# Casting the values on another engine and reordering the first batch of a fused attention and mixer kernel

## The chip, the cores and the metric

The kernel runs on one core of a Trainium2 chip. The metric is the device time of one execution in microseconds (us). The engines are named as in the profile: PE (TensorE, the matrix engine; PEld is its weight load), ACT (ScalarE), DVE (VectorE), POOL (GpSimd) and SP (SyncE, which here only issues transfers). Each engine works through its own instructions in the order in which they were written.

## The reference

For 8 batches of 12 heads, 448 tokens and head size 64:

```python
q_n, k_n = rmsnorm(q, g_q), rmsnorm(k, g_k)
attn = softmax(q_n @ k_n^T / 8)
x    = attn @ v                      # heads side by side: 448 x 768 per batch
u    = x + (x^T @ U @ V)^T           # low-rank mixing over tokens, rank 32
out  = u + relu(u @ w_ch1) @ w_ch2   # 768 -> 3072 -> 768
```

Inputs and output are float32; the kernel multiplies in bfloat16.

## The kernel before, in words

The 12 heads of a batch are worked in three groups of four heads, and a group is two pairs of heads, so a batch has six pairs. Groups are numbered over all batches: groups 0, 1 and 2 are batch 0, group 3 is the first of batch 1. A group goes through these steps:

- `load_qk` and `load_v` (lines 92 to 115) issue its q, k and v loads from SP. Three groups of tiles exist (`stage`, three buffers).
- `squares` (ACT or POOL), `sums` (DVE) and `roots` (ACT: a logarithm and an exponential, lines 169 and 170) make one over the root mean square of each row, in the tile `rs`. `scale` (line 173) multiplies q and k by it and writes `qn` and `kp` in bfloat16. `qn` and `kp` have one buffer each.
- `turn(gi, 0)` and `turn(gi, 1)` transpose `qn` and `kp` on PE (7 transposes each, line 354) into a PSUM tile `pt`. `take_q` and `take_k` (lines 357 and 366) copy them, on DVE, to `qT` and `kT`.
- `values(gi)` (line 199) casts v from float32 to bfloat16: one cast of 128x768 into `va` (line 201) and two of 64x128 into `vl` (line 203).

Then, for each pair, `Sc` (line 401) makes four blocks of scores on PE, r = 0 to 3, and ACT takes their exponential `E` (line 416): three of 128x896 and one of 128x448. Two PSUM tiles are there for scores, so a block can start when the exponential of two blocks earlier has been read. `V` (line 425) multiplies E with `va` and `vl` on PE for one half of the tokens; DVE takes the reciprocal of the row sums and scales the result (lines 444 and 445). In the tables, `V2(i, half)` is V for pair i.

Batch 0 is written out by hand. Its order is the dictionary `extra` (line 607): after each score block (pair, r) come the steps listed there. Ahead of it stand the first steps (lines 748 to 787), which also issue the loads of U, V and of group 3. `keep_busy(n)` issues n small matmuls on PE whose result nobody reads. `weights(n)` issues the next n loads of w_ch1 and w_ch2 from POOL's own queue (`load_w1`, line 276, four parts; then `load_w2`). `mix_t0`, `mix`, `mix_rows` do the low-rank mixing of batch 0; they need `prep_u` and `prep_v` (casts on POOL). All small PSUM tiles (`pt`, `pv`, `busy`, `pu` and others) share four buffers.

From the end of batch 0's attention on, the loop at line 822 takes turns between attention of the later batches (`att`) and the two large matmul stages `up` (line 529) and `down` (line 561), by costs and due times. It counts from the end of batch 0, so that the order of all that follows is the same before and after the change.

## Time and profile before

| what | value |
|---|---|
| median of 3 runs | 588.72 us (587.82 to 588.96) |
| the profiled execution, its time | 588.72 us |
| the profiled execution, its span | 586.8 us |
| PE busy, of the span | 574.6 us (98%) |
| ACT, POOL and DVE busy | 300.1, 213.3 and 197.1 us |
| PE busy from 0 to 44 us | 37.86 us |
| PE busy from 44 us to the end | 536.73 us of 543 |
| granted PE clock | 0.998 |

The span runs from the first to the last instruction; 1.92 us of the time lie around it. The page's first part gives busy time by engine. The timeline gives, for one engine and a window, start, duration, line, tile written and read, and in brackets the idle time before with what ended it; instructions of the same kind are merged ("x3"). Durations of POOL are rough.

### The profile page before, as it was taken

To read this page: it belongs to the slowest core of one execution; us is meant where nothing else is said; L and a number is where in the kernel's file an instruction comes from. 1 tells how busy PE (TensorE), PEld (TensorE's weight loads), DVE (VectorE), ACT (ScalarE), POOL (GpSimd) and SP (SyncE) were. 2 spreads that over 40 slices of the span, in tenths; PEclk is the share of its full clock that TensorE was granted. 3 is DMA by queue.
4 is the path that set the end of the run, shared out by engine and by line. 5 is a ranking of instruction groups with operands and counts; after the bars stand their busy time and mean duration, and the time that the engine had idled before them with its cause. 6 is when DMAs were issued, how large, how long until landed. Compare 5 with 4: busy or idle time off the path is not lost.

```text
span 586.8 us, 11702 instructions
## 1 busy us (share of the span) xinstructions
PE 574.6 (98%) x4826; PEld 334.2 (57%) x4826; DVE 197.1 (34%) x458; ACT 300.1 (51%) x472; POOL 213.3 (36%) x312
## 2 busy tenths in 40 slices
PE   8899999999999999999999999999999999999996
PEld 7655556555565555655566555655556555655563
DVE  6676655312353223521244330641134210410011
ACT  6866650678443774566744568347653254014200
POOL 5995684464044524415153605343352000000000
PEclk9999999999999999999999999999999999999999
DMA  8899999573536641775066732566024110420022
GB/s 222 168 241 241 244 234 220 125 192 75 133 76 170 150 121 26 179 179 124 6 156 105 189 93 55 142 171 146 10 46 103 41 28 1 62 67 1 1 54 55
DMA packets 104509, 68.21 MB, mean 116 GB/s; under 512 B 66568, under 2 KB 101256, under 8 KB 104456
## 3 DMA queue, kind: packets, MB, share of 16 engines
q1 hardware_dynamic: 95044, 58.03, 42.3%
q0 software_dynamic: 9408, 9.44, 9.6%
q8 instruction: 38, 0.62, 0.4%
q14 instruction: 15, 0.12, 0.1%
q10 hardware_dynamic: 4, 0.00, 0.0%
HBM read 52.20 MB, written 11.01 MB: 108 GB/s over the span
## 4 chain that ended last, share of the span: by engine, by line
PE 92%; DMA 3%; ACT 2%; POOL 1%; DVE 1%; issue 1%; SPq 1%; POOLq 0%; ACTq 0%
PE po L561 36%; PE ph L529 36%; PE pv L441 6%; PE sc L415 5%; PE sl L415 2%; PE pv L437 2%; PE pm L512 2%; DMA kf<-in_k_dram 2%; ACT E L416 1%; PE pu L460 1%; DMA qT<-qn 1%; PE pt L354 1%; POOL kp L174 1%; DMA uT<-x 0%; PE sc L547 0%
## 5 line engine op out<-in xcount | busy, mean ns | idle before, releaser
L561 PE MATMUL po<-w2b,hT 128*128 128x384 bf16 x1344 | 237.7, 326 | 0.0
L529 PE MATMUL ph<-uT,w1b 128*128 128x448 bf16 x1140 | 229.4, 352 | 0.0
L416 ACT ACTIVATE E<-sc,gg 128x896 bf16<-128x896 f32 (+1 forms) x150 | 140.1, 988 | 117.4 <-PE sc L415 117.1
L561 PEld LDWEIGHTS <-hT 128*128 128x128 bf16 x1344 | 125.9, 98 | 77.0 <-issue 3.3
L529 PEld LDWEIGHTS <-w1b 128*128 128x128 bf16 x1140 | 107.9, 98 | 95.1 <-issue 3.0
L536 ACT ACTIVATE hT<-ph 128x448 bf16<-128x448 f32 x184 | 98.4, 548 | 122.7 <-PE ph L529 121.9
L444 DVE RECIPROCAL r<-pv 128x4 f32<-128x4 f32 x96 | 17.4, 182 | 185.0 <-PE pv L441 184.7
L193 POOL TENSOR_TENSOR qn<-qf,rs 128x384 bf16<-128x384 f32 x36 | 29.9, 830 | 134.9 <-ACT rs L170 126.8
L386 POOL TENSOR_SCALAR qT<-qT,gg 128x448 bf16<-128x448 bf16 x36 | 50.5, 1402 | 76.4 <-DMA qT<-qn 69.2
L571 DVE TENSOR_TENSOR ob<-po,x 128x384 f32<-128x384 f32 x48 | 26.8, 558 | 102.7 <-PE po L561 101.2
L441 PE MATMUL pv<-va,E 128*128 128x65 bf16 x1152 | 57.1, 194 | 0.0
L441 PEld LDWEIGHTS <-E 128*128 128x128 bf16 x1152 | 50.5, 98 | 6.4
L162 DVE TENSOR_REDUCE ssq<-sq 128x14 f32<-128x896 f32 x45 | 47.0, 1079 | 3.7 <-ACT sq L140 2.9
L415 PE MATMUL sc<-qT,kT 64*128 64x448 bf16 (+1 forms) x294 | 43.3, 354 | 4.2 <-ACT E L416 2.7
L437 PE MATMUL pv<-vl,E 128*128 128x130 bf16 x192 | 42.2, 220 | 0.3 <-ACT E L416 0.2
L445 DVE TENSOR_TENSOR x<-pv,r 128x256 bf16<-128x256 f32 x96 | 40.7, 424 | 3.3
L415 PEld LDWEIGHTS <-kT 64*128 64x128 bf16 (+1 forms) x336 | 14.0, 94 | 42.7 <-issue 39.0
L517 DVE TENSOR_TENSOR x<-pm,x 128x384 bf16<-128x384 f32 x48 | 26.3, 554 | 17.3 <-PE pm L512 15.0
L193 POOL TENSOR_TENSOR kp<-kf,rs 128x384 bf16<-128x384 f32 x36 | 29.8, 828 | 0.0
L416 ACT ACTIVATE E<-sl,gg 128x448 bf16<-128x448 f32 x42 | 26.8, 638 | 0.0
L437 PEld LDWEIGHTS <-E 128*128 128x128 bf16 x192 | 18.7, 97 | 9.8 <-issue 2.0
L571 DVE TENSOR_TENSOR ob<-po,u_rest 128x384 f32<-128x384 f32 x8 | 4.5, 558 | 46.9 <-PE po L561 46.9
(93 smaller groups left out, 321.3 us busy)
## 6 DMA issues: line engine op xcount, KB each, us to landing
qf<-in_q_dram SPq DMA_DIRECT2D x23, 448.0 KB, 3.6
kf<-in_k_dram SPq DMA_DIRECT2D x23, 448.0 KB, 5.3
out_dram<-ob SPq DMA_DIRECT2D x50, 192.0 KB, 2.7
vf<-in_v_dram SPq DMA_DIRECT2D x48, 192.0 KB, 5.3
w1b<-in_moe_w_ch_dram POOLq DMA_DIRECT2D x4, 1152.0 KB, 19.9
w2b<-in_moe_w_ch_dram POOLq DMA_DIRECT2D x8, 576.0 KB, 18.4
vf<-in_v_dram SPq DMA_DIRECT2D x48, 32.0 KB, 4.7
out_dram<-ob SPq DMA_DIRECT2D x12, 96.0 KB, 3.6
```

The lines of the kernel that those rows point to most:

```text
L162: nc.vector.tensor_reduce(ssqs[gi][:, i, :], sqs.pop((gi, i)), AX, ALU.add)
L193: nc.gpsimd.tensor_tensor(main.rearrange("p (t i) d -> p i t d", i=2), src[:, c, :2 * NJ].rearrange("p (i t) d -> p i t d", i=2), rs[:, c, ...
L386: nc.gpsimd.tensor_scalar(qT[:, a], qT[:, a], gg[:, 0:1], None, ALU.mult)
L415: nc.tensor.matmul(sc[:, i, :S], kT[d, keys], qT[d], start=True, stop=True)
L416: nc.scalar.activation(es[(b, pr)][:, 2 * r:2 * r + n, :], sc[:, :n, :S], AF.Exp, scale=scal, bias=bias)
L437: nc.tensor.matmul(pv[:, i].rearrange("p e d -> p (e d)"), E[:, 2 * NJ, w:w + P], vl[:, lp, :], start=True, stop=False)
L441: nc.tensor.matmul(pv[:, i, e, :], E[:, 2 * j + e, w:w + P], va[:, (first_h + step * e) * NJ + j, :], start=False, stop=(e == 1 and j == N ...
L445: nc.vector.tensor_tensor(xs[b].rearrange("p i (h d) -> p i h d", d=D)[:, 2 * half:2 * half + 2, h0:h0 + step + 1:step, :], pv[:, :, :, :D ...
L529: nc.tensor.matmul(ph, w1b[:, dt, ht * P:(ht + 1) * P], uT[:, dt, off:off + S], start=(dt == 0), stop=(dt == KD - 1))
L536: nc.scalar.activation(hT[:, ht, off:off + S], ph, AF.Relu)
L561: nc.tensor.matmul(po, hT[:, ht, col:col + P], w2b[:, ht, half * HALF:(half + 1) * HALF], start=(ht == 0), stop=(ht == KH - 1))
L571: nc.vector.tensor_tensor(ob[:, h], po, urows(b, col, half), ALU.add)
```

## The change

- `values` takes an engine. For groups 0 and 1 it is DVE. Group 0's casts move from POOL, behind `squares(2, 0)`, to DVE, behind `take_k(0, 1)` and ahead of `sums(2, 0)`. Group 1's move from POOL to DVE, behind `sums(2, 1)`.
- `scales(1)` (`roots` and the two `scale` of group 1) and `squares(2, 1)` move one block forward, from (0, 2) to (0, 1), and the first part of w_ch1 is issued there, behind `squares(2, 1)`, in place of (1, 3).
- `turn(1, 0)` and its `take_q` move from (1, 2) to (1, 1), ahead of `V2(0, 0)`; `V2(0, 1)` moves from (1, 3) to (1, 2), ahead of `turn(1, 1)`. At (1, 3) a `keep_busy(6)` is added.
- `turn(2, 0)` stays at (3, 2), `turn(2, 1)` moves to (3, 3), behind that block's scores.
- `squares(3, 0)` moves from (3, 3) to (2, 3), and `prep_u` from (2, 3) to (3, 3).
- q and k of group 3 are issued ahead of U, V and the v of group 2.

```diff
-    def values(gi):
+    def values(gi, eng=nc.gpsimd):
         tv, va, vl = staged[gi][2], *normed[gi][2:]
-        nc.gpsimd.tensor_copy(va[:, :, :D], tv[:, :NM, :])
+        eng.tensor_copy(va[:, :, :D], tv[:, :NM, :])
         for e in range(2):
-            nc.gpsimd.tensor_copy(vl[e * R:(e + 1) * R, :, e * D1:e * D1 + D], tv[e * R:(e + 1) * R, NM:, :])
+            eng.tensor_copy(vl[e * R:(e + 1) * R, :, e * D1:e * D1 + D], tv[e * R:(e + 1) * R, NM:, :])
...
-        (0, 1): [(0, keep_busy, (8,))],
-        (0, 2): scales(1) + [(0, squares, (2, 1, pool)), (0, keep_busy, (8,))],
+        (0, 1): scales(1) + [(0, squares, (2, 1, pool)), (0, weights, (1,)), (0, keep_busy, (8,))],
+        (0, 2): [(0, keep_busy, (8,))],
         (0, 3): [(0, keep_busy, (8,))],
         (1, 0): [(0, keep_busy, (8,))],
-        (1, 1): [V2(0, 0), (0, keep_busy, (6,))],
-        (1, 2): [(0.4, turn, (1, 0)), (0, take_q, (1, 0)), (0, take_q, (1, 1)), (0, keep_busy, (8,))],
-        (1, 3): [(0.4, turn, (1, 1)), (0, take_k, (1, 0)), V2(0, 1), (0, take_k, (1, 1)), (0, sums, (2, 1)),
-                 (0, values, (1,)), (0, load, (4,)), (0, weights, (1,))],
+        (1, 1): [(0.4, turn, (1, 0)), (0, take_q, (1, 0)), (0, take_q, (1, 1)), V2(0, 0), (0, keep_busy, (6,))],
+        (1, 2): [V2(0, 1), (0, keep_busy, (8,))],
+        (1, 3): [(0.4, turn, (1, 1)), (0, take_k, (1, 0)), (0, take_k, (1, 1)), (0, sums, (2, 1)),
+                 (0, values, (1, nc.vector)), (0, load, (4,)), (0, keep_busy, (6,))],
         (2, 1): scales(2) + [(0, weights, (1,)), V2(1, 0)],
         (2, 2): [(0, keep_busy, (6,))],
-        (2, 3): [V2(1, 1), (0, prep_u, ())],
+        (2, 3): [V2(1, 1), (0, squares, (3, 0, pool))],
...
-        (3, 2): turns(2),
-        (3, 3): [V2(2, 1), (0, take_k, (2, 1)), (0, squares, (3, 0, pool)), (0, values, (2,)), (0, load, (5,)),
-                 (0, weights, (1,)), (0, prep_v, (0, 1)), (0, squares, (3, 1, pool)), (0, weights, (1,))],
+        (3, 2): [(0.4, turn, (2, 0)), (0, take_q, (2, 0)), (0, take_q, (2, 1))],
+        (3, 3): [(0.4, turn, (2, 1)), (0, take_k, (2, 0)), V2(2, 1), (0, take_k, (2, 1)), (0, values, (2,)), (0, load, (5,)),
+                 (0, prep_u, ()), (0, weights, (1,)), (0, prep_v, (0, 1)), (0, squares, (3, 1, pool)), (0, weights, (1,))],
...
-    values(0)
...
     take_k(0, 1)
+    values(0, nc.vector)
     sums(2, 0)
     stage_tiles(3)
+    load_qk(3, 0)
+    load_qk(3, 1)
     load_u()
     load_v(2)
-    load_qk(3, 0)
-    load_qk(3, 1)
     load_v(3)
```

## The prediction

> **What bounds the kernel now.** I read the busy time by engine first, then the same cut at 44 us, then the timelines of ACT and POOL from 12 to 37 us, and the waits.

> ```profile
> PE 574.6 (98%) x4826; PEld 334.2 (57%) x4826; DVE 197.1 (34%) x458; ACT 300.1 (51%) x472; POOL 213.3 (36%) x312
> ```

> ```profile
> 0.00:44.00 44.00, 37.86 (x486) 27.70 (x487) 28.94 (x87) 31.88 (x49) 35.86 (x52) 1.00 0.93 210
> 44.00:587.00 543.00, 536.73 (x4342) 306.54 (x4340) 168.15 (x371) 268.26 (x423) 177.40 (x261) 1.00 0.49 109
> ```

> After 44 us PE is busy 536.73 of the 542.8 us left in the span (the clock is 1.00 throughout), and the order there is unchanged. So what the change is worth is how much sooner or later batch 0's attention ends; the rest follows. In batch 0 ACT leads, and these are its exponentials (starts, durations, in brackets what it waited for):

> ```profile
> 12.26 2.79 ACT L416 ACTIVATE E<-sc,gg 128x896 bf16<-128x896 f32 x3
> 14.93 0.32 ACT L169 ACTIVATE rs<-ssq,eps 128x28 f32<-128x28 f32 x1
> 15.28 0.23 ACT L170 ACTIVATE rs<-rs 128x28 f32<-128x28 f32 x1
> 15.41 3.31 ACT L416 ACTIVATE E<-sc,gg 128x448 bf16<-128x448 f32 x4
> 19.02 0.64 ACT L416 ACTIVATE E<-sc,gg 128x448 bf16<-128x448 f32 x1 [0.30 <-PE sc L415]
> 20.91 1.90 ACT L416 ACTIVATE E<-sc,gg 128x896 bf16<-128x896 f32 x2 [1.26 <-PE sc L415]
> 23.08 0.32 ACT L169 ACTIVATE rs<-ssq,eps 128x28 f32<-128x28 f32 x1 [0.26 <-DVE ssq L162]
> ...
> 28.82 4.32 ACT L416 ACTIVATE E<-sc,gg 128x896 bf16<-128x896 f32 x5 [0.22 <-PE sc L415]
> ```

> The idle times add up to 2.6 us until 36 us; no reordering of batch 0 that leaves ACT's work alone can win more. The largest, 1.26 us, ends with the scores of pair 2, which wait for group 1's keys. Those come from POOL, which hardly pauses:

> ```profile
> 12.93 1.68 POOL L143 TENSOR_TENSOR uT<-qf 128x896 f32<-128x896 f32 x1 [3.71 <-DMA qf<-in_q_dram]
> 14.55 0.83 POOL L201 CAST va<-vf 128x768 bf16<-128x768 f32 x1
> 15.32 0.64 POOL L203 CAST vl<-vf 64x128 bf16<-64x128 f32 x2
> 16.04 1.69 POOL L174 TENSOR_TENSOR qn<-qf,rs 128x896 bf16<-128x896 f32 x1
> 17.69 1.69 POOL L174 TENSOR_TENSOR kp<-kf,rs 128x896 bf16<-128x896 f32 x1
> 19.33 1.68 POOL L143 TENSOR_TENSOR sq<-kf 128x896 f32<-128x896 f32 x1
> ```

> **The change, part by part.** Pair 1, block 2 is written (1,2).

> *Roots of group 1 one block sooner.* Exponentials are 0.895 apart (2.79 for three that overlap), so the logarithm starts at 14.04 instead of 14.93 and rs is done at 14.62 (0.58 later, as 14.93 to 15.51). E(0,2) gives way by 0.48 and E(0,3) is back on its old time, 15.41. POOL can start qn at 14.76 (0.14 after rs, as 23.66 to 23.80 later on) instead of 16.04.

> *Casts on DVE.* On POOL they took 1.43 per group. No row shows DVE casting from SBUF to SBUF. Its copies of bfloat16 from PSUM (0.36 for 384 elements, 0.81 for two of 448) go at some 0.55 ns an element, its casts of float32 (0.69 for 512) at 1.04. So va takes 0.57 to 0.96, each vl 0.23 to 0.26, a group 1.0 to 1.5 us. DVE is free from 14.16 (after k's copies) and next wanted at 17.1, so a group's 1.5 plus the 1.09 of `sums(2, 0)` would fit. v has landed: 9.3 us after its issues of 4.24 and 5.4, 8.2 after those of 6.39 and 7.1.

> *What the casts meet.* They now run beside POOL's back-to-back work. Two places show POOL beside a DVE operation that both reads and writes full rows in SBUF:

> ```profile
> 6.43 1.83 POOL L156 TENSOR_TENSOR qn<-qf,rs 128x512 bf16<-128x512 f32 x2
> 7.96 1.31 DVE L156 TENSOR_TENSOR kp<-kf,rs 128x512 bf16<-128x512 f32 x2 [0.15 <-ACT rs L170]
> ```

> ```profile
> 40.83 1.08 DVE L174 TENSOR_TENSOR kp<-kf,rs 128x896 bf16<-128x896 f32 x1
> 41.70 1.76 POOL L174 TENSOR_TENSOR qn<-qf,rs 128x896 bf16<-128x896 f32 x1
> ```

> By line L156's own durations DVE took 845 ns for 512 elements and 547 for 384. With 896 in 1081 an element costs 1.04 ns, so 512 should take 680: it lost 165, having started 0.30 before POOL ended at 8.26. At 41.70 POOL took 1757 where its others of that form took 1677 to 1689: it lost 70, having started 0.21 before DVE ended. Each time the later one is held until the other is done, less some 0.14 of start-up. Against it: DVE's sums (L162, one input, 14 results) run 1.09 beside POOL's casts and hold nobody. The cast lies between: one input, but full rows written. I take it as held, since the two rows share with it that full rows are read and written in SBUF; the free case is the other end of the range. Held, the casts come in turns: va waits for the square (done 14.61, let go about 14.55) and runs to 15.1; qn, waiting since 14.76, then runs to 15.1 + 1.69 - 0.14 = 16.65; the first vl to 16.85; kp to 18.45; the second vl to 18.65.

> [...]

> *What then follows on PE.* `turn(1, 0)` runs at 16.7. `V2(0, 0)` behind it needs vl: 18.7 (it started at 16.45). It and six fillers take 0.86 (16.45 to 17.31), the scores reach ACT 0.41 later: E(1,2) at 19.95 instead of 17.72. On DVE `sums(2, 0)` and two `take_q` stand behind vl: 18.65 + 1.09 + 0.81 = 20.55. The eight fillers take the buffer that `take_q` frees: 20.55 + 0.44 = 21.0, then Sc(1,3), `turn(1, 1)` at 21.2, k's first copy 0.60 later (19.43 to 20.03) at 21.8, after the two normalisations (1.2 from 20.55). Sc(2,0) comes 0.42 after that and E(2,0) another 0.46: 22.65 instead of 20.91, **+1.75**. The added `keep_busy(6)` (0.34) lies beside that copy.

> *Given back.* The old E(2,1) was followed by 0.38 of waiting for `sums(2, 1)` (23.08 against 20.91 + 1.79). Now the sums start at 21.8 + 1.35 and end at 24.25, ahead of 22.65 + 1.79 = 24.45. E(2,2) is at 24.93 instead of 23.56, **+1.37**. Group 1's casts follow the sums, 24.25 to 25.2, before POOL's next qn gets going at 25.3. POOL then ends kp of group 2 at 28.5 (old 27.13). Sc(3,3) stands ahead of `turn(2, 1)`, so E(3,3) loses its 0.17 wait, but E(4,0) needs that turning at 28.55, 1.37 late, and DVE's queue is 0.08 shorter: E(4,0) at 30.1 instead of 28.82, **+1.3**. From there the order is old and nothing waits anew.

> *Transfers and POOL's other moves.* q and k of group 3 add two issues of 0.47 on SP ahead of U, V and v of group 2, at 15.46, where the transfer engines are 0.28 and 0.13 busy (16 to 18, 18 to 20 us). v of group 2 landed 6.8 to 7.2 us after issues up to 20.7; 0.93 later is 28.9, and POOL casts it at 31.0 (29.2 in the free case). `squares(3, 0)` loses its 0.54 wait for q. `prep_u` now ends near 33.0, for a matmul that wants it at 33.3. The first w1 issue (1.05) still stands ahead of group 2's scaling, which waits for roots anyway; it landed 14.9 us after 22.31, before its first use at 37.88, and now comes 2 us sooner. All this I cost at nothing; uncovered, v would cost up to 0.3 and `prep_u` up to 0.6.

> **Sum.** Against the profiled execution, 588.72 us (span 586.8 and 1.92 around it; it is the median): 588.72 + 1.3 = **590.0 us**.

> **Rivals.** *A, the casts hold nobody* (the side of no loss). For it: sums beside POOL lose nothing. qn ends at 16.44, `turn(1, 0)` and the longer PE row put E(1,2) at 18.26 and E(2,0) at 20.86; the sums no longer wait, so E(2,2) gains 0.43, E(3,3) another 0.28, E(4,0) ends 0.52 ahead: 588.2. It decides if vl is ready when PE reaches `V2(0, 0)` at 17.0. *B, held, but DVE's three casts go through together.* POOL's qn starts at 15.5, ends at 17.05, E(2,0) is 0.44 late, and the missing waits bring it back: 588.8. Against it: POOL waits already from 14.76. *D, DVE gets no turn* until POOL leaves its rows at 19.7: vl at 20.7, all of the forecast 2.1 later: 592.1. Against it: at 41.70 and 7.96 the waiting one came next.

> **Chances.** Forecast 0.47, A 0.24, B 0.18, D 0.11. What a measurement of this kernel tells from no change is about 0.2%, 1.18 us. The forecast's steps are good to some 0.5, with unmodelled hand-overs only adding, so 0.65 of it lies above 1.18: slower 0.31 + 0.11 + 0.02 of B = 0.44. Faster by that much needs over twice A's gain, and ACT's idle time sets the limit: 0.05. Same 0.51. Range 587.8 (A, 0.4 better) to 591.2 (forecast, 1.2 worse), which leaves out D.

> **What would show it.** Held: POOL's qn near 1.9 to 2.0 instead of 1.69 or the two vl apart by a whole POOL instruction; `V2(0, 0)` waiting for DVE; E(2,0) after 22. A: vl done by 15.7 and qn and kp at 1.69; E(4,0) near 28.3. Wrong altogether: a difference that arises after 44 us.

## The result, and the profile after

The changed kernel took **589.09 us** (median of 22 runs, 588.50 to 593.41). The kernel before, on the same chip, took 588.41 us (22 runs, 586.91 to 589.86). The ratio is **1.0025, with a 95% interval of 1.0014 to 1.0035**. By medians the change costs 0.68 us, by means 1.22 us (589.60 against 588.38), because four of the 22 executions lie at 591.24 to 593.41. The forecast was 590.0 with a range of 587.8 to 591.2, and a chance of 0.51 for a change within 0.2%; by the medians it came out that way (0.68 us is 0.12%), while the interval of the ratio lies on both sides of 0.2%.

The profiled execution of the changed kernel took 588.76 us (span 587.0), the one of before 588.72 (span 586.8). The same cut at 44 us as before, for the kernel after (the columns are length, then busy time of PE, PEld, DVE, ACT and POOL, granted clock, DMA share, GB/s):

```profile
0.00:44.00 44.00, 37.62 (x485) 27.96 (x487) 32.73 (x92) 31.41 (x48) 33.05 (x45) 1.00 1.00 228
44.00:587.00 543.00, 537.73 (x4348) 307.01 (x4345) 168.65 (x372) 268.99 (x424) 178.80 (x262) 1.00 0.48 107
```

PE has 1.00 us more to do after 44 us than before (537.73 against 536.73): the first batch ended that much later. Nearly as much came back further on. The stretch from 100 to 120 us, with the same columns, in the kernel before:

```profile
100.00:120.00 20.00, 19.20 (x148) 10.34 (x147) 8.32 (x15) 13.06 (x20) 11.27 (x15) 1.00 0.67 150
```

PE's timeline of the kernel before has its one gap of that stretch:

```profile
117.20 0.56 PE L415 MATMUL sc<-qT,kT 64*128 64x448 bf16 x4 [0.80 <-POOL qT L386]
```

And the same stretch in the kernel after:

```profile
100.00:120.00 20.00, 20.00 (x158) 10.93 (x156) 8.82 (x17) 12.68 (x19) 8.31 (x13) 1.00 0.70 154
```

Before, PE waited 0.80 us for a copy on POOL, from 116.4 on; after the change it is busy throughout. So +1.0 early and -0.8 late make the +0.2 of these two executions.

Now the first batch. The timeline of DVE after the change, from the copies of k to the sums of group 2 (start, duration, instruction):

```profile
14.49 0.56 DVE L201 CAST va<-vf 128x768 bf16<-128x768 f32 x1
14.97 3.36 DVE L203 CAST vl<-vf 64x128 bf16<-64x128 f32 x2
18.36 1.09 DVE L162 TENSOR_REDUCE ssq<-uT 128x14 f32<-128x896 f32 x1
...
23.94 0.55 DVE L201 CAST va<-vf 128x768 bf16<-128x768 f32 x1
24.41 0.47 DVE L203 CAST vl<-vf 64x128 bf16<-64x128 f32 x2
```

Group 1's casts at 24 us run while POOL does nothing: two `vl` in 0.47 us. Group 0's two at 14.97 take 3.36 us. POOL at the same time:

```profile
14.52 2.08 POOL L174 TENSOR_TENSOR qn<-qf,rs 128x896 bf16<-128x896 f32 x1 [1.98 <-DVE kT L372]
16.56 1.69 POOL L174 TENSOR_TENSOR kp<-kf,rs 128x896 bf16<-128x896 f32 x1
18.20 1.68 POOL L143 TENSOR_TENSOR sq<-kf 128x896 f32<-128x896 f32 x1
```

`qn` takes 2.08 instead of 1.69, ends when the first `vl` gets its turn, and the second `vl` ends at 18.33, just after `kp` is done (18.25). The time held is shown here as busy, not as waiting (2.08 instead of 1.69 for `qn`, 1.71 and 1.62 for the two `vl` instead of 0.47 together); only the durations tell. PE stands behind it (kernel after):

```profile
16.65 0.56 PE L354 MATMUL pt<-ident,qn 128*128 128x128 bf16 x7
18.38 0.22 PE L437 MATMUL pv<-vl,E 128*128 128x130 bf16 x1 [1.16 <-DVE vl L203]
```

And the exponentials on ACT, to be read against those of before:

```profile
11.84 1.91 ACT L416 ACTIVATE E<-sc,gg 128x896 bf16<-128x896 f32 x2
13.81 0.32 ACT L169 ACTIVATE rs<-ssq,eps 128x28 f32<-128x28 f32 x1
...
19.70 1.01 ACT L416 ACTIVATE E<-sc,gg 128x896 bf16<-128x896 f32 x1 [2.06 <-PE sc L415]
21.18 0.63 ACT L416 ACTIVATE E<-sc,gg 128x448 bf16<-128x448 f32 x1 [0.46 <-PE sc L415]
22.45 1.91 ACT L416 ACTIVATE E<-sc,gg 128x896 bf16<-128x896 f32 x2 [0.64 <-PE sc L415]
24.24 0.32 ACT L169 ACTIVATE rs<-ssq,eps 128x28 f32<-128x28 f32 x1
...
29.89 1.91 ACT L416 ACTIVATE E<-sc,gg 128x896 bf16<-128x896 f32 x2 [0.39 <-PE sc L415]
```

The first exponential came at 11.84 here and at 12.26 in the execution of before, because a transfer landed sooner. So below, times of the first batch are also given from the first exponential on: E(4,0), the first exponential of pair 4, is 18.05 after it, instead of 16.56.

### The profile page after: what moved, and what is told of

Same layout as the page of the kernel before. It is cut to its first block, busy times and chain, and to the rows that moved or that the text cites. A ratio compares the mean times of both kernels' runs of the same rounds, so it can differ in the third digit from the quotient of the medians.

```text
span 587.0 us, 11709 instructions
## 1 busy us (share of the span) xinstructions
PE 575.4 (98%) x4831; PEld 335.0 (57%) x4832; DVE 201.4 (34%) x464; ACT 300.4 (51%) x472; POOL 211.8 (36%) x306
## 4 chain that ended last, share of the span: by engine, by line
PE 94%; DVE 2%; ACT 2%; DMA 1%; issue 0%; SPq 0%; ACTq 0%
PE po L561 37%; PE ph L529 37%; PE pv L441 6%; PE sc L415 6%; PE sl L415 2%; PE pv L437 2%; PE pm L512 2%; ACT E L416 1%; PE pt L354 1%; DMA kf<-in_k_dram 1%; PE pu L460 1%; DVE vl L203 1%; DVE ssq L162 1%; PE busy L240 0%; PE sc L547 0%
## 5 line engine op out<-in xcount | busy, mean ns | idle before, releaser
L416 ACT ACTIVATE E<-sc,gg 128x896 bf16<-128x896 f32 (+1 forms) x150 | 140.3, 990 | 118.9 <-PE sc L415 118.5
L162 DVE TENSOR_REDUCE ssq<-sq 128x14 f32<-128x896 f32 x45 | 46.8, 1079 | 3.1 <-ACT sq L140 3.0
L415 PE MATMUL sc<-qT,kT 64*128 64x448 bf16 (+1 forms) x294 | 43.2, 355 | 3.1 <-ACT E L416 2.4
L415 PEld LDWEIGHTS <-kT 64*128 64x128 bf16 (+1 forms) x336 | 13.8, 94 | 41.8 <-issue 38.8
L416 ACT ACTIVATE E<-sl,gg 128x448 bf16<-128x448 f32 x42 | 26.9, 640 | 0.0
L437 PEld LDWEIGHTS <-E 128*128 128x128 bf16 x192 | 18.7, 97 | 9.8 <-issue 2.0
## 6 DMA issues: line engine op xcount, KB each, us to landing
w1b<-in_moe_w_ch_dram POOLq DMA_DIRECT2D x4, 1152.0 KB, 16.4
```

Source lines behind the costliest of these rows:

```text
L162: nc.vector.tensor_reduce(ssqs[gi][:, i, :], sqs.pop((gi, i)), AX, ALU.add)
L415: nc.tensor.matmul(sc[:, i, :S], kT[d, keys], qT[d], start=True, stop=True)
L416: nc.scalar.activation(es[(b, pr)][:, 2 * r:2 * r + n, :], sc[:, :n, :S], AF.Exp, scale=scal, bias=bias)
L437: nc.tensor.matmul(pv[:, i].rearrange("p e d -> p (e d)"), E[:, 2 * NJ, w:w + P], vl[:, lp, :], start=True, stop=False)
```

## The experiments

Four things had to be told apart: the casts' turns with POOL, the order of the loads, the place of `prep_u`, and the roots and turnings. In the table, "ratio" is to the kernel before on the same chip, and the last column is E(4,0) minus the first exponential in the profiled execution. e1 to e4 ran on one chip (median of before 588.16), e5 to e8 and e9 to e11 on another (588.22, then 588.00) and e12 on a third (588.47), so a difference of medians across these groups can be off by some 0.3 us, and more against e12.

| Kernel | median (lowest to highest) us | ratio [95%] | E(4,0) |
|---|---|---|---|
| before | 588.41 (586.91 to 589.86) | | 16.56 |
| after | 589.09 (588.50 to 593.41) | 1.0025 [1.0014, 1.0035] | 18.05 |
| e1 casts with one input | 589.92 (586.85 to 592.88) | 1.0037 [1.0016, 1.0058] | 16.30 |
| e2 before + loads | 587.15 (586.98 to 587.79) | 0.9985 [0.9977, 0.9994] | 16.18 |
| e3 after, old loads | 589.07 (588.61 to 593.22) | 1.0029 [1.0013, 1.0046] | 18.06 |
| e4 after, gap filled | 589.14 (589.02 to 592.29) | 1.0024 [1.0011, 1.0037] | 18.54 |
| e5 after, `prep_u` back | 588.79 (588.40 to 590.06) | 1.0012 [1.0002, 1.0023] | 18.06 |
| e6 e1, `prep_u` back | 587.17 (586.88 to 589.17) | 0.9990 [0.9979, 1.0002] | 16.31 |
| e7 e5, `vl` on POOL | 587.30 (587.08 to 588.63) | 0.9987 [0.9977, 0.9997] | 16.48 |
| e8 before + `prep_u` moved | 587.99 (586.99 to 589.77) | 0.9998 [0.9988, 1.0008] | 16.18 |
| e9 after, v of group 2 later | 594.58 (590.55 to 597.12) | 1.0116 [1.0075, 1.0157] | 19.26 |
| e10 e5, v of group 2 later | 593.28 (590.93 to 595.24) | 1.0089 [1.0065, 1.0113] | 18.05 |
| e11 e6, old turnings | 587.04 (586.81 to 588.94) | 0.9990 [0.9975, 1.0005] | 16.18 |
| e12 e1, fillers before `pu` | 589.02 (587.79 to 593.21) | 1.0023 [1.0004, 1.0042] | 16.30 |

The 16.56 of the kernel before is that of a late execution. Its POOL waits 3.71 us for q of group 2 (the row at 12.93 in the prediction) and starts `qn` of group 1 3.78 after the first exponential. In e2 and e8, whose order of work up to there is the same, it waits 2.05 and 2.50 and starts `qn` 3.40 after it, and E(4,0) comes at 16.18 in both.

### e1: the casts as sums over one element

DVE makes the same casts as a reduction over an axis of length 1, the operation of `sums`.

```diff
+        def cast(dst, src):
+            if eng is nc.vector:
...
+                    nc.vector.tensor_reduce(dst, src.rearrange("p j d -> p j d ()"), AX, ALU.add)
+            else:
+                eng.tensor_copy(dst, src)
-        eng.tensor_copy(va[:, :, :D], tv[:, :NM, :])
+        cast(va[:, :, :D], tv[:, :NM, :])
...
-            eng.tensor_copy(vl[e * R:(e + 1) * R, :, e * D1:e * D1 + D], tv[e * R:(e + 1) * R, NM:, :])
+            cast(vl[e * R:(e + 1) * R, :, e * D1:e * D1 + D], tv[e * R:(e + 1) * R, NM:, :])
```

> The changed kernel with one difference: DVE casts the values of groups 0 and 1 as a sum over an axis of length one, an operation with one input that showed no holding beside POOL (line L162). Its price by the reductions of 896 in 1.08 us: va about 0.95, each vl about 0.29 us. Theory 1 (DVE's cast and POOL's operations exclude each other, in turns): nothing is held, qn of group 1 takes 1.69 us instead of 2.08, the last vl is done 2.5 us sooner, the scores of pair 2 reach ACT 8.6 us after the first exponential (changed kernel 10.6, kernel before 8.65), E(4,0) 16.0 us after it (18.05 and 16.56). The time is then 0.5 us (0.1%) below the kernel before, or 1.3 (0.2%) if the wait at 116 us stays away too. Theory 2 (the loss comes from the longer rows of PE and DVE, whatever the cast does): E(4,0) stays 18 us after the first exponential and the time stays 0.25% above the kernel before.

In its first 30 us it did what was expected: no wait at `V2(0, 0)`, POOL's `qn` at 1.69, E(4,0) at 16.30 (16.0 was expected; 18 if the casts had not been the cause). The total did not follow: 589.92, with a spread of 6 us. Its profiled execution (590.93 us) shows why. PE, from the scores of 30.94 on:

```profile
30.94 0.37 PE L421 MATMUL sc<-qT,kT 64*128 64x448 bf16 x2 [0.55 <-ACT E L422]
32.70 1.89 PE L481 MATMUL pu<-x 128*128 128x512 bf16 x4 [1.39 <-POOL x L333]
34.51 0.56 PE L421 MATMUL sc<-qT,kT 64*128 64x448 bf16 x2
```

PE waits 1.39 us for `prep_u` (its cast `x`), and then the same scores take 0.56 instead of 0.37. `prep_u` was late because it now stands behind `values(2)`, and POOL waited there for v:

```profile
29.29 0.82 POOL L206 CAST va<-vf 128x768 bf16<-128x768 f32 x1 [0.25 <-DMA vf<-in_v_dram]
30.83 0.29 POOL L206 CAST vl<-vf 64x128 bf16<-64x128 f32 x1 [0.72 <-DMA vf<-in_v_dram]
31.72 0.29 POOL L206 CAST vl<-vf 64x128 bf16<-64x128 f32 x1 [0.60 <-DMA vf<-in_v_dram]
32.08 0.32 POOL L332 CAST Ub<-x 128x160 bf16<-128x160 f32 x1
32.34 0.29 POOL L333 CAST x<-x 128x128 bf16<-128x128 f32 x1
```

The granted clock of this execution, cut where it changes (the column after the five busy times):

```profile
28.63:32.04 3.41, 1.86 (x21) 0.92 (x19) 2.56 (x8) 3.41 (x5) 1.81 (x4) 1.00 1.14 242
32.04:35.46 3.42, 2.77 (x14) 1.00 (x15) 0.69 (x1) 0.72 (x2) 3.38 (x6) 0.50 1.13 251
35.46:38.87 3.41, 3.41 (x34) 2.25 (x32) 1.76 (x5) 1.84 (x3) 3.32 (x5) 0.50 1.14 242
38.87:42.00 3.13, 3.13 (x54) 2.48 (x53) 2.74 (x8) 1.42 (x3) 3.09 (x6) 1.00 1.13 240
```

Half the clock for 6.83 us, from 32.04 to 38.87, loses up to 3.4 us (half of 6.83, an estimate). In this kernel, the part of the change that the prediction had costed at nothing was worth more than the part it had worked out.

### e2 and e3: the loads alone, and all but the loads

```diff
+    load_qk(3, 0)
+    load_qk(3, 1)
     load_u()
     load_v(2)
-    load_qk(3, 0)
-    load_qk(3, 1)
```

e2 is the kernel before with this edit; e3 is the changed kernel without it.

> The kernel before with one difference: q and k of group 3 are issued ahead of U, V and the v of group 2. Theory 3 (the earlier loads fill idle transfer time at 16 to 20 us, all later loads land sooner, and the 0.80 us for which PE waits at 116 us goes): batch 0 as before (E(4,0) 16.6 us after the first exponential), the last half of w_ch2 lands some 4 us sooner than 97.7, no wait at 116 us, time 0.8 us (0.14%) below the kernel before. Rival (that wait is a matter of when PE comes by, not of the loads): the wait stays between 0.5 and 0.9 us and the time is the same.

> The changed kernel with the loads in the old order. Theory 3 (the loads took away the wait at 116 us): the wait is back, 0.3 to 0.8 us, and the time is 0.3 to 0.8 us above the changed kernel, 0.3 to 0.4% above the kernel before. Rival (PE now comes 1.1 us later to the same transfers, and so waits no longer): no wait at 116 us, the time that of the changed kernel.

e2 gains 1.01 us by medians, the only single part of the change that gains. Its executions lie within 0.8 us of each other, while those of before on the same chip reach from 586.97 to 589.77. The best of before are as good as e2, so what the order of the loads removes is something that only some executions have. The wait of 0.80 at 116 us is one such thing: of all the profiled executions only that of the kernel before has it. It is also missing in e3 and in e8, which load in the old order, so a single trace cannot tell how often it comes, and which transfer decides it was not isolated. Nor is it the whole difference between the two traces: 0.70 us is there already at E(4,0) (28.82 before, 28.12 in e2; 0.32 of it at the first exponential), and e8, with the old order of loads, has 27.93. That the median gains 1.0 us is shown; by what way is not. e3 equals the changed kernel (589.07 and 589.09): when the first batch is late anyway, the sooner loads buy nothing more. In e3's profiled execution (592.52) POOL starts the squares of group 3 at 30.57 after 1.60 of idle time (29.15 and none in the changed kernel; their q is issued at 20.67 instead of 13.17, but the trace names a copy on DVE as what ended the wait), `prep_u` is late, and PE waits 1.33 us for it, with half the clock behind it again (0.68 in the mean from 30 to 40 us).

### e4: the pause of 1.16 us filled

```diff
-        (1, 1): [(0.4, turn, (1, 0)), (0, take_q, (1, 0)), (0, take_q, (1, 1)), V2(0, 0), (0, keep_busy, (6,))],
+        (1, 1): [(0.4, turn, (1, 0)), (0, take_q, (1, 0)), (0, take_q, (1, 1)), (0, keep_busy, (20,)), V2(0, 0), (0, keep_busy, (6,))],
```

> The changed kernel with 20 more filler matmuls ahead of the first V, in the 1.16 us for which PE waits for vl. Theory 4 (that pause lets the granted clock fall in some executions: 4 of 22 took 591.2 to 593.4 us at a mean clock of 0.993 to 0.997, the others 588.5 to 589.9): the median stays at 588.5 to 589.1, no execution is above 590.5 and the mean falls by 0.5 us. Rival (the long executions have another cause): some are still above 591, at a clock of 0.997 or less.

The median did not move (589.14), one of 11 executions was still long (592.29), and E(4,0) came 0.49 later, since the fillers outlast the wait. We took this as speaking against Theory 4. It was too early, as e9 shows: there the clock fell to 0.50 after a pause of 1.17 us, while it stayed at 1.00 after the 1.16 of the changed kernel's profiled execution.

### e5, e6, e7, e8: the place of prep_u, and the casts without it

e5 undoes this part of the change; e6 and e7 do so on top of other forms of the casts; e8 makes this part alone, in the kernel before. In the changed kernel:

```diff
-        (2, 3): [V2(1, 1), (0, squares, (3, 0, pool))],
+        (2, 3): [V2(1, 1), (0, prep_u, ())],
...
-        (3, 3): [(0.4, turn, (2, 1)), (0, take_k, (2, 0)), V2(2, 1), (0, take_k, (2, 1)), (0, values, (2,)), (0, load, (5,)),
-                 (0, prep_u, ()), (0, weights, (1,)), (0, prep_v, (0, 1)), (0, squares, (3, 1, pool)), (0, weights, (1,))],
+        (3, 3): [(0.4, turn, (2, 1)), (0, take_k, (2, 0)), V2(2, 1), (0, take_k, (2, 1)), (0, squares, (3, 0, pool)), (0, values, (2,)),
+                 (0, load, (5,)), (0, weights, (1,)), (0, prep_v, (0, 1)), (0, squares, (3, 1, pool)), (0, weights, (1,))],
```

> The changed kernel with prep_u back in (2,3) and the squares of q of group 3 back in (3,3), behind take_k(2,1); everything else as changed. Theory 5 (the changed kernel's long executions, 4 of 22 above 591, come from prep_u, which now stands behind values(2) on POOL: when v of group 2 lands late, PE waits some 1.3 us at the first pu matmul and is then held at half clock for 6.83 us, 3.4 us lost): none of some 11 executions above 590.3; median 588.9, since the ordinary executions keep the casts' turns (+1.3) and the gain of the earlier loads (-0.8). Rival (the long executions come from something else, such as the pause of 1.16 us at 17 us): one to three of 11 above 591, as before.

> The casts on DVE as sums over an axis of length 1 (as in the run e1_cast_one_input, where POOL was not held and the logarithm of group 2 came at 22.44 instead of 24.24), and prep_u back in (2,3). Theory 1 with theory 5: no cast waits for POOL, E(4,0) comes at most 16.6 after the first exponential, the wait of 0.80 at 116 us is gone, and no execution is pulled up by a late prep_u: median 587.0 (588.4 - 0.8 - 0.6), all of them below 588.5. Rival (the spread of e1, 586.9 to 592.9, had another cause): a spread of several us again and a median near 589.5.

> The changed kernel with only the large cast va on DVE, the two small casts vl on POOL ahead of its scaling, and prep_u back in (2,3). Theory 1: the loss is the two small casts standing a whole POOL instruction each; without that va is done near 15.1, POOL does vl by 15.3 and the scaled keys are done near 18.6 as in the changed kernel, but PE has vl early, so E(1,2) comes near 18.3 and E(2,0) near 21.4, E(4,0) some 0.3 later than before relative to the first exponential: median 588.0. Rival (it is POOL's order, not DVE's standing, that costs): E(2,0) near 22.4 and 588.9.

> The kernel before with one edit: prep_u moves from (2,3) to (3,3), behind values(2), and the squares of q of group 3 from (3,3) to (2,3), as in the changed kernel; loads and casts stay. Theory 5: median within 0.4 us of before, with one to four of 11 executions 2 to 4 us longer, and in such a one a wait of over 1 us on POOL's prep_u at the first pu matmul near 32 us. Rival (prep_u's place is harmless by itself): all executions within those of before, below 590.

e5 and e6 came as Theory 5 said: 588.79 and 587.17, none of e5's eleven above 590.1 (which alone shows little: with 4 of 22 long ones in the changed kernel, a set of 11 would have none in about one case of six), and of e6's twelve only two a little above the 588.5 that was set (588.58 and 589.17). Against e1, e6 differs in the place of `prep_u` alone (and of the squares that it changed places with): seven of e1's ten executions are above 589.5, none of e6's twelve. Between e5 and e6 only the form of the casts differs, and that is **1.62 us**. DVE in e6:

```profile
14.52 0.95 DVE L204 TENSOR_REDUCE va<-vf 128x768 bf16<-128x768 f32 x1
15.39 0.58 DVE L204 TENSOR_REDUCE vl<-vf 64x128 bf16<-64x128 f32 x2
```

and POOL in e6:

```profile
14.54 1.69 POOL L174 TENSOR_TENSOR qn<-qf,rs 128x896 bf16<-128x896 f32 x1 [2.05 <-DVE kT L378]
16.18 1.69 POOL L174 TENSOR_TENSOR kp<-kf,rs 128x896 bf16<-128x896 f32 x1
```

The slower operation (0.95 instead of 0.56 for `va`) holds nobody and is held by nobody, and the three are done at 15.97 instead of 18.33. e7 keeps `va` as a cast on DVE and puts `vl` back on POOL, where it runs in a wait that POOL has anyway; `qn` again takes 2.08 behind `va`, and nothing else is held. POOL in e7:

```profile
13.79 0.64 POOL L203 CAST vl<-vf 64x128 bf16<-64x128 f32 x2 [0.31 <-DMA vf<-in_v_dram]
15.19 2.08 POOL L174 TENSOR_TENSOR qn<-qf,rs 128x896 bf16<-128x896 f32 x1 [0.76 <-DVE kT L372]
```

We had expected 588.0 and it took 587.30, with E(2,0) 9.04 after the first exponential instead of e5's 10.62 (8.87 in e6). So it was the two small casts, each standing behind a whole POOL instruction (1.71 and 1.62 us in the changed kernel), that cost, and hardly `va`.

e8 went by the rival. PE did wait for `prep_u` in its profiled execution:

```profile
31.92 1.04 PE L475 MATMUL pu<-x 128*128 128x512 bf16 x3 [0.77 <-POOL x L327]
```

but the clock stayed (1.00 until 120 us), and none of 12 executions was longer than the longest of before. In these runs the place of `prep_u` hurt where v of group 2 came later (e1, where POOL waits for it) or POOL came later to `prep_u` (e3: its cast starts at 33.93, against 31.57 in e8).

### e9 and e10: v of group 2 later still

```diff
     load_u()
+    load_v(3)
     load_v(2)
-    load_v(3)
```

e9 is the changed kernel with this edit, e10 is e5 with it.

> The changed kernel with v of group 3 loaded ahead of v of group 2, so that v of group 2 lands about 1 us later. Theory 5 (prep_u behind values(2) on POOL had 0.23 us to spare in the profiled execution of the changed kernel: done at 32.81, PE at 33.04): prep_u ends near 33.8 or later, PE waits about 1 us or more at the first pu matmul, and in most executions the granted clock falls to half for 6.83 us after it: median above 591, most executions 591 to 594. Rival (a late prep_u costs no more than its own wait): PE waits the same, the clock stays, median 589.8 to 590.3.

> The same late v of group 2, with prep_u back in (2,3), ahead of values(2), and the squares of q of group 3 in (3,3). Theory 5: PE does not wait for prep_u, the values of group 2 have time until PE reaches pair 4's weighted sums near 36 us: median 588.8 as in e5_prep_back, none above 590.5. Rival (late values of group 2 hurt by another way, for instance the squares of k of group 3 behind them): a wait of PE between 33 and 42 us, and a median above 589.5.

e9 took 594.58, as Theory 5 wanted and longer than it said, with three of five above 594. v was delayed by more than the 1 us that both expectations put down: on SP the issues of v of group 2 start at 21.10 in e9 and 22.04 in e10, against 18.65 in the changed kernel. In e9's profiled execution (592.89) PE waits 1.40 us for `prep_u`, and the clock falls (0.50 from 35.53 to 38.94); but it had fallen once before, after the pause that e4 filled. PE there:

```profile
18.47 0.27 PE L437 MATMUL pv<-vl,E 128*128 128x130 bf16 x1 [1.17 <-DVE vl L203]
```

The windows of e9 around it, cut where the clock falls and comes back, and 3.41 us ahead of that:

```profile
15.05:18.46 3.41, 1.78 (x19) 1.09 (x19) 3.35 (x4) 2.68 (x4) 3.41 (x3) 1.00 1.01 299
18.46:21.87 3.41, 3.40 (x41) 2.82 (x41) 2.58 (x6) 1.01 (x1) 2.51 (x2) 0.50 0.66 125
```

The same pause is in the profiled execution of the changed kernel, whose intervals of 3.41 us, counted from its first begin of full clock at 6.02, begin at another point of the work:

```profile
16.26:19.67 3.41, 2.14 (x33) 1.45 (x34) 3.33 (x4) 1.38 (x2) 3.41 (x3) 1.00 0.72 227
19.67:23.08 3.41, 3.22 (x54) 2.41 (x55) 3.05 (x13) 2.27 (x3) 1.21 (x2) 1.00 0.79 162
```

PE is idle for 3.41 - 1.78 = 1.63 us (1.64 before rounding) in the one, and the clock falls for the next interval; for 1.27 us in the other, and it stays. In e9 E(4,0) is 1.21 later for it. So Theory 4 held in e9, where the interval caught the whole pause together with 0.37 of the 0.66 that PE waits from 14.76 to 15.42, and did not show in this execution of the changed kernel.

e10 went by its rival (593.28): the late values themselves held PE. POOL stood 4.00, 0.40 and 1.00 us for the parts of v and cast the last at 38.06. PE in e10:

```profile
38.41 0.27 PE L437 MATMUL pv<-vl,E 128*128 128x130 bf16 x1 [3.82 <-POOL vl L203]
```

So e10 cannot say what `prep_u`'s place is worth with so late a v; e6 against e1 can for the loads as changed. What e9 and e10 add is how far the landing moves: with the same order of loads and issues 0.9 to 1.4 us apart, the last part of v was cast from 34.8 on in e9 and from 38.06 on in e10. The margin of 0.23 us that `prep_u` had in the changed kernel's profiled execution (done at 32.81, wanted at 33.04) says little of another execution.

### e11: the old turnings

e6, with pair 1's `turn`, `take_q`, `take_k` and `V2` in the order of the kernel before, and without the added `keep_busy(6)`; the roots stay a block sooner.

```diff
-        (1, 1): [(0.4, turn, (1, 0)), (0, take_q, (1, 0)), (0, take_q, (1, 1)), V2(0, 0), (0, keep_busy, (6,))],
-        (1, 2): [V2(0, 1), (0, keep_busy, (8,))],
+        (1, 1): [V2(0, 0), (0, keep_busy, (6,))],
+        (1, 2): [(0.4, turn, (1, 0)), (0, take_q, (1, 0)), (0, take_q, (1, 1)), (0, keep_busy, (8,))],
...
+        (1, 3): [(0.4, turn, (1, 1)), (0, take_k, (1, 0)), V2(0, 1), (0, take_k, (1, 1)), (0, sums, (2, 1)),
+                 (0, values, (1, nc.vector)), (0, load, (4,))],
```

> As e6_one_input_prep_back (casts as one-input sums on DVE, prep_u in its old place, loads and roots sooner), but pair 1's turnings and V2 in the order of the kernel before: V2(0,0) alone in (1,1), the first turning of group 1 in (1,2), the second and V2(0,1) in (1,3). Theory 6 (the roots' gain of 1.3 us on POOL is real, and is given back by the turning put ahead of V2(0,0), which makes E(1,2) 0.9 us later than before): E(1,2) near 5.5 after the first exponential instead of 6.38, the scaled keys near 18.1, E(2,0) near 7.8 instead of 8.87, E(4,0) near 15.6 instead of 16.31: median 586.5. Rival (ACT's own work and the sums of group 2 are the limit): E(4,0) between 16.1 and 16.4 and a median of 587.1, the same as e2 and e6.

The rival held: E(4,0) at 16.18, 587.04 us. E(1,2) came at 5.97, sooner than e6's 6.38, and the next logarithm's sums took the gain back. The sooner roots (with the casts off POOL) and the turnings are worth nothing either way here: e2, e6 and e11 all take 587.0 to 587.2. These and e7 beat both kernels, by 0.10 to 0.15% against before; that is under the 0.2% from which the prediction took a measurement to tell, though the intervals of e2 and e7 end below 1.

### e12: fillers ahead of the late pu

```diff
-        (5, 0): [(0.9, mix_t0, (0, 512))],
+        (5, 0): [(0, keep_busy, (16,)), (0.9, mix_t0, (0, 512))],
```

on e1, where `prep_u` is late.

> The kernel of e1_cast_one_input (prep_u in its new place, where it is late), with 16 fillers of 128x128 on PE directly ahead of the first pu matmul, about 0.9 us at full clock. Theory 7 (the granted clock falls to half for whole intervals of 3.41 us, whose start differs from execution to execution, when PE's idle time adds up to more than some 1.4 us inside the interval before: 1.55, 1.55, 1.64, 1.94 and 3.13 us in the profiled executions where it fell, at most 1.35 where it stayed): the wait of 1.4 us shrinks to about 0.5, the sum in an interval to about 1.3 or less, no execution shows a mean clock below 0.997, and the long ones go: median 588.2 (e6's 587.17, up to 0.9 for the fillers where prep_u is in time, and what is left of the wait), none above 590, although prep_u is as late as in e1. Rival (the long executions of e1 are the lateness itself, not the clock): the spread of e1, 587 to 593 with a median near 590, stays.

This is half a result. The median is 0.9 lower (589.92 to 589.02, on another chip; the ratio went from 1.0037 to 1.0023), and eight of twelve executions lie below 589.7, but four are still at 591.3 to 593.2, with mean clocks of 0.997 to 0.994, where Theory 7 wanted none above 590. The profiled execution is a short one (587.80): the fillers take 1.07 us, cover the whole wait, and PE is idle 0.92 us in the interval. Whether v was later than the fillers reach in the four long ones, no trace shows, so that the clock alone makes the long executions stays unproven.

## Why the prediction was right, and what it left out

*Roots of group 1 one block sooner*: right. The logarithm starts 1.97 after the first exponential; the step had 1.78.

*Casts on DVE*: right, at the lower end of its bounds: `va` 0.56 (0.57 to 0.96 was put), `vl` 0.23 to 0.24 each where nothing holds them.

*What the casts meet*: right, in kind and order. From the first exponential on, the second `vl` was to end at 6.39 and did at 6.49. Rival D is out, since the waiting one always came next; B, since three casts never went through together; A, since POOL and DVE do hold each other (`qn` 2.08 instead of 1.69, the two `vl` 3.36 instead of 0.47). For casts that hold nobody A forecast E(4,0) 16.04 after the first exponential, and e6, where they do not, has 16.31. The two rows with two inputs were the right neighbours for the cast.

That the casts hold POOL, and POOL them, is shown for these instructions: by the 2.08 us of `qn` behind `va`, in the changed kernel and in e7, by the 1.71 and 1.62 of the two `vl`, and by 1.62 us of total between the cast (e5) and the reduction (e6), beside which `qn` takes 1.69. What makes them hold each other, no run shows.

*What then follows on PE* and *Given back*: right to 0.2 us. E(2,0) 10.61 after the first exponential (10.39 was put), E(4,0) 18.05 (17.84). The forecast +1.3 became +1.49 in this pair of traces. But the starting point, 16.56, was that of a late execution: against e2 or e8, with 16.18, E(4,0) is +1.87. The time that belongs to it is the 1.62 between e5 and e6 (1.75 apart at E(4,0)), or 1.64 between e5 and e2.

*Transfers and POOL's other moves*, costed at nothing, is the step that failed, on both sides. The sooner loads gain about 1.0 us in the kernel before (e2), for which the step had no term: we never asked what the wait of 0.80 at 116 us, which the trace of before does show, depends on. In the pair of traces that wait is gone, so of the 1.0 us lost before 44 us only 0.2 reach the end; the prediction had all of it do so ("the rest follows"). Its own sign, "Wrong altogether: a difference that arises after 44 us", did happen in that respect. And the place of `prep_u`, put at up to 0.6 if uncovered, costs 0.30 on the median between the changed kernel and e5, and 0.62 on the mean (589.60 against 588.98); between e1 and e6 it costs 2.75 and 2.63. What was missing is the clock: in e1 a late `prep_u` costs its wait of 1.39 us and then up to 3.4 us (estimated) by the clock of 0.50 for 6.83 us.

The sum of the parts, by medians and along one path through the experiments: loads -1.0 (before to e2), roots and turnings 0.0 (e2 to e6), casts held +1.6 (e6 to e5), `prep_u` +0.3 (e5 to the changed kernel), together +0.9; measured +0.7, forecast +1.3. The parts do not simply add: with the casts held, the sooner loads gain nothing (e3 and the changed kernel take the same). On this path the forecast had the casts 0.3 and `prep_u` 0.3 too low and left out a gain of 1.0, so that errors of opposite sign cancelled in part. That the total came so near is in part luck.

What remains open: how the four executions above 591 divide. One interval of 3.41 us at half clock takes 0.003 from the mean clock of such an execution (half of 3.41 in 587), two take 0.006, so the two of them with a mean of 0.997 (591.24 and 591.73) hold one at most; the other two have 0.995 and 0.993. Nor is every long execution one of the clock: a run of the kernel before, beside e9 to e11, took 591.03 with a mean clock of 1.000. Four more of the changed kernel's 22 lie at 589.71 to 589.89 with a mean clock of 0.997, and two of e5's 11 at 590.06 with the same clock; this fits one interval at half clock after the pause at 17 us (+1.21 in e9). In e5 a late `prep_u` cannot be the cause, as `prep_u` stands early there; in the changed kernel it is not excluded. No trace of such an execution of the changed kernel itself was had.

## What to carry to other kernels

A small cast put on DVE beside a busy POOL cost here not its 0.2 us but a whole POOL instruction of 1.69, and the profile showed the wait as busy time (1.71 and 1.62 us for the two): compare the duration with the same form elsewhere, and use a form that holds nobody (here a one-element reduction), or the wait that POOL has anyway. Every move that is costed at nothing because something covers it should carry its margin in us, and the spread of the transfer it hangs on: 0.23 us was no cover for a load whose last part was cast from 34.8 us on in e9 and from 38.06 on in e10. And on PE the idle times of one stretch are to be added up: with 1.55 us or more of idle time in an interval of 3.41, the price here was no longer the wait alone.

## What the runs showed of the hardware

It had not been expected either that a form of the same cast, at 0.95 us instead of 0.56, would be the faster one by 1.62 us of total time.
